# Making two decay tables on chip and reordering the first three blocks of a fused retention, mixture-of-experts and gated-MLP kernel

## Chip, cores and metric

One core of one Trainium2 chip. The metric is the device time of one launch in microseconds (us), the median of several runs. Three runs of the kernel before stand at the start of this case; the profile comes from one more execution.

## What is computed

Three stages, all float32, for 4 batches of 576 positions. Only the first matters here:

```python
scores = q @ k.T / sqrt(64)                       # 8 heads of 64
gamma  = 1 - 2.0 ** (-5 - arange(8))              # one decay per head
D      = where(t >= s, gamma ** (t - s), 0)       # causal decay mask
x      = (scores * D) @ v                         # then the heads side by side: 512 columns
# x -> top-1 mixture of experts (routing by x) -> gated MLP with a spatial product -> out
```

## The kernel before, in words

The first stage works on 16 blocks of 128 positions: block `j` is chunk `j // 4` of batch `j % 4`. (The last 64 positions of each batch come afterwards.) Each block is one tile of 128 x 2048 floats, loaded in two halves of 512 KB: first q and k (`blk[:, 0:1024]`), then k by rows and v. I call these halves a and b. Loads are issued on SP (SyncE's queue) by `load_blk`, and there are five block buffers (`bp`, tag "blk", line 271). The Tile framework puts the waits in.

For block `j` the steps are

- `scaled` (line 401, POOL): the keys times a table `ktab` (`kt`), and from chunk 1 on the queries times a table `q1`, `q2` or `q3` (`qh`);
- `scores` (line 370, PE): 16 small float32 products into the one PSUM tile `sc`. Every float32 product stands in the trace as two records, so these are 32;
- `masked` (line 391, DVE): two multiplications of `sc` by the mask table `dtab` (128 x 1024 floats, powers of gamma times 0.125 under the causal mask), giving `pm`;
- `state_products` and `score_products` (lines 466 and 476, PE): the running state times `qh`, and `pm` times v, into PSUM tile `oT`. For chunk 0 there is no state, and `state_products` issues nothing;
- `evict` (line 497, ACT): `oT` to `xT` in SBUF;
- `state_update` (line 412): PE products of `kt` and v into PSUM tile `st`, and DVE's addition to the state `Sbd`;
- `turn` (line 508, PE): `xT` times an identity beside the routing weights (`iw`) into PSUM tile `tx`; `logits` (DVE) and `keep` (ACT) read it.

The loop at line 777 sets the order. PE's order is exactly the order of the calls (`manual_schedule` for PE only); the orders on DVE, ACT, POOL and SP in this stretch are chosen by the framework's planner. In step `j` of the loop PE does `scores(j)`, `state_products(j-1)`, then `state_update(j-2)` and `turn(j-2)`, then `score_products(j-1)`. So the masked scores of a block have one step to be made before they are used. `routing` (line 604 and on) is fed in between by `advance`; after block 15 the routing of the last blocks ends the stage, and the expert products (lines 1179 to 1181) start at 114.37 us.

`small_constants` (line 329), called in step 1, loads a tile `CS` and copies ten small tables from it on DVE. `keep_warm` (line 252) issues bf16 products of a zero tile; seven of them stand ahead of the loop. The constant tables `dtab`, `q1` and the others are computed on the host into one array `cst`, and `load_c` loads a column range of it.

Of the kernel before, what the change touches and what calls it, by code (L numbers as in the profile page):

```python
# [8 lines left out]
F32 = mybir.dt.float32  # L9
# [5 lines left out]
ALU = mybir.AluOpType  # L15
# [4 lines left out]
B, H, S, DH = 4, 8, 576, 64  # L20
# [4 lines left out]
P = 128  # L25
NBLK = 18
TW = P + 9
# [4 lines left out]
EC = 256  # L32
HC = EC + CAPS[0]
GATE_TH = -1.788e-7
WARM = (4, 2, 3, 3)
FILL = (8, 3, 30, 48)
ET = mybir.EngineType
# [4 lines left out]
LPOOL = (1, 4, 6)  # L42

_CONST_LAYOUT = [
    ("dtab", H * P), ("q1", 4 * P), ("q2", 4 * P), ("q3", 4 * P), ("q4", 4 * P),
    ("late", H * 64),
    ("ktab", 4 * H), ("ident", P), ("jmat", 64), ("halfm", 2), ("first", 1), ("rest", 1), ("e8", 8),
    ("mless", 32), ("mmore", 32), ("rbase", 1), ("sel4", 4), ("i32", 32),
# [7 lines left out]
    _o += _w  # L56
CW = _o
SMALL0 = COFF["ident"][0]


def shape_constants(caps):
    c = np.zeros((P, CW), np.float64)

    def put(name, a, rows=P):
        o, w = COFF[name]
        c[:rows, o:o + w] = np.asarray(a, np.float64).reshape(rows, w)

    gam = 1.0 - 2.0 ** (-5.0 - np.arange(H))
    i = np.arange(P)
    rel = i[None, :] - i[:, None]  # L70
    dt = np.zeros((P, H, P))
    for h in range(H):
        g = np.where(rel >= 0, gam[h] ** np.maximum(rel, 0), 0.0) * 0.125
        dt[:, (h % 2) * 4 + h // 2] = np.roll(g, 64 * (h // 2 % 2), axis=0)
    put("dtab", dt)
    kt = np.zeros((P, 4, H))
    for cc in range(4):
        for h in range(H):
            kt[:, cc, h] = gam[h] ** (512.0 - cc * P - np.roll(i, 64 * (h // 2 % 2)))
    put("ktab", kt)  # L80
    qt = np.zeros((P, 3, 4, P))
    late = np.zeros((P, 2, 4, 64))
    q4 = np.zeros((P, 4, P))
    for pr in range(4):
        for hh in range(2):
            g = gam[2 * pr + hh]
            for cc in range(1, 4):
                qt[hh * 64:(hh + 1) * 64, cc - 1, pr, :] = 0.125 * g ** (cc * P + i - 512.0)
            late[:, hh, pr] = np.where(np.arange(64)[None, :] >= (i % 64)[:, None], g ** -(i % 64.0)[:, None], 0.0)
            q4[(hh ^ pr % 2) * 64:(hh ^ pr % 2) * 64 + 64, pr] = 0.125 * g ** (i % 64.0)  # L90
    for cc in range(3):
        put(f"q{cc + 1}", qt[:, cc])
    put("q4", q4)
    put("late", late)
    put("ident", np.eye(P))
    put("jmat", (i[:, None] % 64) == np.arange(64)[None, :])
    put("halfm", np.stack([i < 64, i >= 64], 1))
    put("first", (i == 0))
    put("rest", (i > 0))
    put("e8", np.tile(8.0 - np.arange(8), (P, 1)))  # L100
    rb, re = np.arange(32) // 8, np.arange(32) % 8
    same_e = re[:, None] == re[None, :]
    put("mless", same_e * (rb[:, None] < rb[None, :]), 32)
    put("mmore", same_e * (rb[:, None] > rb[None, :]), 32)
    put("rbase", RS * re - 1.0, 32)
    put("sel4", rb[:, None] == np.arange(4)[None, :], 32)
    put("i32", np.eye(32), 32)
    put("esum", re[:, None] == np.arange(8)[None, :], 32)
    put("row0", np.tile(RS * np.arange(8.0) - 1.0, (P, 1)))
    put("seq", np.tile(np.asarray(SEQ, np.float64), (P, 1)))  # L110
    put("iota_pb", np.arange(4)[None, :] * P + i[:, None] + 1.0)
    put("iota_bk", np.tile(np.arange(20.0) * P, (P, 1)))
    put("iota_p", i)
    put("caps", np.tile(np.asarray(caps, np.float64), (P, 1)))
    return c.astype(np.float32)


def lay_out(q, k, v, moe_w_gate, moe_w_local, moe_w1, moe_w2,
# [21 lines left out]
    for b in range(4):  # L140
# [14 lines left out]
    ws[64:, 4] = wt[512:]  # L155
    wo = moe2_w_out.reshape(4, P, 512).transpose(1, 0, 2).reshape(P, 2048)
    bs = np.tile(moe2_b_spatial[None, :], (P, 1))
    r = dict(blk=blk, lat=lat, wgl=wgl.reshape(P, 4 * TW), w1=w1, w2=w2, wv=wv, wu=wu,
             ws=ws.reshape(P, 5 * S), wo=wo, bs=bs, cst=shape_constants(caps))
    r = {n: np.ascontiguousarray(a) for n, a in r.items()}  # L160
    return {n: a.view(np.int64) if a.dtype == np.float64 else a for n, a in r.items()}


def fused(tc, blk, lat, wgl, w1, w2, wv, wu, ws, wo, bs, cst, out, dbg=None, stop=9, caps=CAPS):
    nc = tc.nc
    V, A, G, T, SP = nc.vector, nc.scalar, nc.gpsimd, nc.tensor, nc.sync
    top = ExitStack()
    with top:
# [100 lines left out]
        with ExitStack() as ph1:  # L269
# [22 lines left out]
                    SP.dma_start(out=ST[i][hf][oth].rearrange("p h c -> p (h c)"), in_=lat[i, oth, 1536:])  # L292

            CS = c1.tile([P, CW - SMALL0], F32, name="CS")
            CB = {n: c1.tile([P, COFF[n][1]], F32, name=f"c_{n}") for n in ("dtab", "q2", "late", "ktab")}
            iw = c1.tile([P, 4, TW], F32, name="iw")
            MV = [[c1.tile([P, H, DH], F32, name=f"mv{i}_{hf}") for hf in range(2)] for i in range(2)]
            LQ = [c1.tile([P, 1024], F32, name=f"lq{i}") for i in range(2)]
# [8 lines left out]
            def load_c(name):  # L307
# [2 lines left out]
                    CB[name] = c1.tile([P, w], F32, name="c_q")  # L310
                SP.dma_start(out=CB[name], in_=cst[:, o:o + w])

            load_blk(0, ((0, 1024),))
            load_c("dtab")
            load_blk(0, ((1024, BLKW),))
            load_c("ktab")
            load_blk(1, ((0, 1024),))
# [73 lines left out]
            def masked(j):  # L391
                d = blks[j]
                sc = d["sc"]
                tab = cs("dtab").rearrange("p (k a t) -> p k a t", k=2, a=4)
                d["pm"] = []
                for hh in range(2):
                    pm = wk.tile([P, 4, P], F32, name=f"pm{hh}")
                    V.tensor_tensor(pm, sc[:, hh], tab[:, hh], op=ALU.mult)  # L398
                    d["pm"].append(pm)

            def scaled(j):
                d = blks[j]
                if d["c"] > 0:
                    d["qh"] = wk.tile([P, 4, P], F32, name="qh", tag="qh")
                    tab = cs(f"q{d['c']}").rearrange("p (a t) -> p a t", a=4)
                    G.tensor_tensor(d["qh"], d["q"], tab, op=ALU.mult)
                kt = wk.tile([P, H, DH], F32, name="kt", bufs=3)
                ktb = cs("ktab").rearrange("p (c h) -> p c h", c=4)[:, d["c"]]
                G.tensor_tensor(kt, d["kk"], ktb[:, :, None].to_broadcast([P, H, DH]), op=ALU.mult)
                d["kt"] = kt  # L410
# [361 lines left out]
            order = tc.manual_schedule(engines={mybir.EngineType.PE})  # L772
            order.__enter__()
            V.memset(zb, 0.0)
            for n in range(7):
                keep_warm(sc_[:, n % 2], 1)
            for j in range(16):
                if j == 14:
                    order.__exit__(None, None, None)
# [5 lines left out]
                    load_late((j - 10) // 2)  # L785
                if j == 1:
                    small_constants()
                if j in (2, 5, 10, 11):
                    load_c({2: "q1", 5: "q2", 10: "q3", 11: "late"}[j])
                if j == 14:  # L790
                    for u in range(4):
                        load_w(u)
                views(j)
                scaled(j)
                scores(j)
                if j > 0:
                    state_products(j - 1)
                masked(j)
                advance()
                if j > 1:  # L800
                    state_update(j - 2)
                    turn(j - 2)
                    logits(j - 2)
                    keep(j - 2)
                    if j in (12, 13):
                        move_state(j - 10)
                    if j == 15:
                        round_w(0)
                        rest_w(0, G)
                if j > 1 and (j - 1) % 4 == 0:  # L810
                    steps.append(routing((j - 5) // 4))
                    advance()
                if j > 0:
                    score_products(j - 1)
                    evict(j - 1)
                advance()
# [739 lines left out]
        order.__exit__(None, None, None)  # L1556


_INS = ["blk", "lat", "wgl", "w1", "w2", "wv", "wu", "ws", "wo", "bs", "cst"]


# [16 lines left out]
```

## Time and profile before

| | |
|---|---|
| three runs, median (lowest to highest) | 562.27 us (560.90 to 562.31) |
| the profiled execution: its time, its span | 561.66 us, 559.9 us |
| instructions | 11740 |
| bytes read from and written to HBM | 77.34 MB, 18.91 MB |
| first stage, up to the first expert product | 114.37 us of the span |
| bytes moved in the first 110 us | 29.84 MB |

The span is what the profiler recorded from the first instruction to the last; the 1.8 us that the execution's time is longer lie around it. In timeline rows the columns are: start in us, duration in us, engine, line, operation, output and inputs with shapes, number of instructions merged into the row, and in brackets the idle time of the engine ahead of it and what ended it. "issue" there means that the profile shows nothing that the engine waited for. PE is the matmul side of TensorE, PEld its weight loads, SPq the loads issued by SP.

### The profile page before, as it was taken

The page shows a single profiled execution, that of the slowest core. Times are in us where ns is not written, and L with a number is a line of the kernel's source. Part 1 is how long each engine was busy: PE and PEld are TensorE (multiplying, and loading weights), DVE is VectorE, ACT ScalarE, POOL GpSimd, SP SyncE. Part 2 cuts the span into 40 slices and gives each one's busy share as a digit, 9 for nine tenths or more (in the row PEclk, how much of TensorE's full clock was granted, in tenths as well). Part 3 has the DMA queues.
Part 4 walks back from the last instruction along what each step waited for, and adds up shares of the span by engine and source line. Part 5 has one row for each costly group of instructions (what it writes and reads, how often), then busy time and mean ns, then how long its engine had stood idle before and what let it go on. Part 6 is the DMA issues. An engine that isn't in the chain of part 4 may idle for free.

```text
span 559.9 us, 11740 instructions
## 1 busy us (share of the span) xinstructions
PE 538.2 (96%) x4629; PEld 491.7 (88%) x4630; DVE 337.0 (60%) x713; ACT 223.4 (40%) x450; POOL 215.9 (39%) x176
## 2 busy tenths in 40 slices
PE   6898899899999999999999999999999899999997
PEld 4787777899999999999999998888888899889986
DVE  1566576533376778698875437996642846666510
ACT  1233243144455544555555542223333523662322
POOL 2566738445134636675635311322004244522000
PEclk9999999999999999999999999999999899999999
DMA  8989953537465474665565514353425553642022
GB/s 295 404 259 373 348 188 108 199 113 240 152 207 180 144 258 157 225 198 192 185 208 157 187 54 113 114 166 124 155 82 174 174 148 107 196 157 77 1 76 94
DMA packets 34059, 97.83 MB, mean 175 GB/s; under 512 B 5604, under 2 KB 5988, under 8 KB 34000
## 3 DMA queue, kind: packets, MB, share of 16 engines
q1 hardware_dynamic: 27696, 77.27, 41.2%
q0 software_dynamic: 5984, 19.24, 11.2%
q8 instruction: 37, 0.61, 0.5%
q10 hardware_dynamic: 320, 0.52, 0.3%
q14 instruction: 22, 0.18, 0.1%
HBM read 77.34 MB, written 18.91 MB: 172 GB/s over the span
## 4 chain that ended last, share of the span: by engine, by line
PE 69%; DVE 5%; ACT 2%; DMA 1%; issue 1%; POOL 0%; ACTq 0%; POOLq 0%; DVEq 0%; SPq 0%
PE acc L1179 12%; PE acc L1180 11%; PE acc L1181 11%; PE acc L1271 11%; PE acc L1273 11%; PE acc L1272 10%; PE tp L1157 1%; DVE wL L245 1%; PE tp L1439 1%; DMA vL<-z_v,yidx 1%; DVE ec L1009 1%; PE acc L1456 1%; PE acc L1455 1%; DVE hL L1198 1%; DVE bigL L1476 0%
## 5 line engine op out<-in xcount | busy, mean ns | idle before, releaser
L245 POOL TENSOR_TENSOR wL<-wst,wH 128x1024 fp32r<-128x1024 f32 x25 | 63.4, 2537 | 60.1 <-ACT wH L241 60.0
L1179 PE MATMUL acc<-hH,wH 128*128 128x416 f32 (+7 forms) x256 | 79.3, 310 | 0.1
L1180 PE MATMUL acc<-hL,wH 128*128 128x416 f32 (+7 forms) x256 | 78.0, 305 | 1.3 <-DVE hL L1198 1.3
L1181 PE MATMUL acc<-hH,wL 128*128 128x416 f32 (+7 forms) x256 | 77.9, 304 | 0.0
L245 DVE TENSOR_TENSOR wL<-wst,wH 128x1024 fp32r<-128x1024 f32 x39 | 52.3, 1342 | 39.3 <-ACT wH L241 38.3
L1180 PE MATMUL acc<-xL,wH 128*128 128x344 f32 (+6 forms) x224 | 66.7, 298 | 0.0
L1181 PE MATMUL acc<-xH,wL 128*128 128x344 f32 (+6 forms) x224 | 66.7, 298 | 0.0
L1179 PE MATMUL acc<-xH,wH 128*128 128x344 f32 (+6 forms) x224 | 66.5, 297 | 0.0
L241 ACT CAST wH<-wst 128x1024 fp32r<-128x1024 f32 x64 | 65.1, 1052 | 1.5 <-DMA wst<-in_w 1.5
L1180 PEld LDWEIGHTS acc<-hL,wH 128*128 128x128 f32 x256 | 48.2, 188 | 1.7 <-DVE hL L1198 1.7
L1179 PEld LDWEIGHTS acc<-hH,wH 128*128 128x128 f32 x256 | 48.2, 188 | 0.5 <-ACT hH L1197 0.3
L1181 PEld LDWEIGHTS acc<-hH,wL 128*128 128x128 f32 x256 | 48.1, 188 | 0.0
L1179 PEld LDWEIGHTS acc<-xH,wH 128*128 128x128 f32 x224 | 42.1, 188 | 0.0
L1181 PEld LDWEIGHTS acc<-xH,wL 128*128 128x128 f32 x224 | 42.1, 188 | 0.0
L1180 PEld LDWEIGHTS acc<-xL,wH 128*128 128x128 f32 x224 | 42.1, 188 | 0.0
L1271 PE MATMUL acc<-wsH,vH 128*128 128x288 f32 x128 | 39.0, 304 | 1.8 <-ACT ze L1383 1.7
L1273 PE MATMUL acc<-wsH,vL 128*128 128x288 f32 x128 | 38.4, 300 | 0.0
L1272 PE MATMUL acc<-wsL,vH 128*128 128x288 f32 x128 | 38.4, 300 | 0.0
L1197 ACT ACTIVATE hH<-acc 128x160 fp32r<-128x160 f32 (+7 forms) x64 | 24.8, 400 | 31.4 <-PE acc L1181 31.2
L1198 DVE SCALAR_TENSOR_TENSOR hL<-acc,hH 128x160 fp32r<-128x160 f32 (+7 forms) x64 | 27.5, 440 | 14.1 <-ACT hH L1197 13.6
L1276 POOL DMA_INDIRECT vL<-z_v,yidx x18 | 17.6, 980 | 44.8 <-DMA z_v<-ze 40.4
L398 DVE TENSOR_TENSOR pm<-sc,c_dtab 128x512 f32<-128x512 f32 x32 | 20.6, 685 | 22.7 <-PE sc L376 22.7
(286 smaller groups left out, 1314.9 us busy)
## 6 DMA issues: line engine op xcount, KB each, us to landing
wst<-in_w SPq DMA_DIRECT2D x64, 512.0 KB, 3.6
blk<-in_blk SPq DMA_DIRECT2D x32, 512.0 KB, 8.5
z_v<-ze SPq DMA_DIRECT2D x18, 257.0 KB, 2.8
z_u<-ze SPq DMA_DIRECT2D x18, 256.0 KB, 2.4
out<-ob SPq DMA_DIRECT2D x15, 256.0 KB, 2.0
raw<-in_wv SPq DMA_DIRECT2D x4, 512.0 KB, 5.0
raw<-in_wu SPq DMA_DIRECT2D x4, 512.0 KB, 5.1
raw<-in_wo SPq DMA_DIRECT2D x4, 512.0 KB, 5.2
```

What stands on the lines that cost most here:

```text
L241: A.copy(wts[u][0], stages[u])
L245: eng.tensor_tensor(wL, stages.pop(u), wH.bitcast(F32), op=ALU.subtract)
L398: V.tensor_tensor(pm, sc[:, hh], tab[:, hh], op=ALU.mult)
L1179: T.matmul(acc, lhsT=wH, rhs=xH, start=first, stop=False)
L1180: T.matmul(acc, lhsT=wH, rhs=xL, start=False, stop=False)
L1181: T.matmul(acc, lhsT=wL, rhs=xH, start=False, stop=last)
L1197: A.activation(hH[:, cols], acc[:, :C], AF.Relu)
L1198: V.scalar_tensor_tensor(hL[:, cols], acc[:, :C], 0.0, hH[:, cols].bitcast(F32), op0=ALU.max, op1=ALU.subtract)
L1271: T.matmul(acc, lhsT=lH, rhs=rH, start=first, stop=False)
L1272: T.matmul(acc, lhsT=lH, rhs=rL, start=False, stop=False)
L1273: T.matmul(acc, lhsT=lL, rhs=rH, start=False, stop=last)
L1276: G.indirect_dma_start(out=t.bitcast(F32), out_offset=None, in_=src[:], in_offset=bass.IndirectOffsetOnAxis(ap=yidx[:, j:j + 1], axis=0))
```

## The change

On chip: the mask table `dtab` and the query table `q1` are no longer loaded. A tile of 8 rows (one per head) and 1792 columns, `rt8`, holds powers of gamma and 0/1 selectors; it is loaded first, into one of the five block buffers, and a 128 x 64 tile of zeros and ones (`mask`) is loaded after the first half of block 0. Eight float32 products of 8 rows make gamma^(t-s) in PSUM; four DVE multiplications by `mask` and two ACT copies carry it into a `dtab` tile that POOL has set to zero. In step 1 four products make `q1`, which ACT copies out.

Order: four instead of seven `keep_warm` ahead of the loop; then block 0 is carried up to `evict` in step 0 (with seven and one `keep_warm` around its products), and its state update, `turn`, `logits` and `keep` move from step 2 to step 1. From block 1 on, the products stay where they were.

```diff
-    ("dtab", H * P), ("q1", 4 * P), ("q2", 4 * P), ("q3", 4 * P), ("q4", 4 * P),
+    ("mask", 64), ("q2", 4 * P), ("q3", 4 * P), ("q4", 4 * P),
...
+TROW = H * P + 512 + 256
...
+def row_tables():
+    gam = 1.0 - 2.0 ** (-5.0 - np.arange(H))
+    i = np.arange(P)
+    t = np.zeros((H, TROW), np.float64)
+    keys, sel = t[:, :H * P].reshape(H, H, P), t[:, H * P:H * P + 512].reshape(H, 4, 2, 64)
+    for h in range(H):
+        keys[h, h] = gam[h] ** -np.roll(i, 64 * (h // 2 % 2)).astype(np.float64)
+        sel[h, h // 2, h % 2] = 1
+    t[:, -256:-128] = 0.125 * gam[:, None] ** i[None, :]
+    t[:, -128:] = 0.125 * gam[:, None] ** (P + i[None, :] - 512.0)
+    return t.astype(np.float32)
...
+            rt8 = bp.tile([P, BLKW], F32, name="rt8", tag="blk")[:H, :TROW]
+            SP.dma_start(out=rt8, in_=rowt)
             load_blk(0, ((0, 1024),))
-            load_c("dtab")
+            load_c("mask")
             load_blk(0, ((1024, BLKW),))
...
             V.memset(zb, 0.0)
-            for n in range(7):
+            dtab = c1.tile([P, H * P], F32, name="dtab")
+            q1 = c1.tile([P, 4 * P], F32, name="c_q")
+            G.memset(dtab, 0.0)
+            for n in range(START[0]):
                 keep_warm(sc_[:, n % 2], 1)
+            dt = psc.tile([P, 2, 512], F32, name="oT")
+            for h in range(H):
+                T.matmul(dt[:, h % 2, h // 2 * P:(h // 2 + 1) * P], lhsT=rt8[:, h * P:(h + 1) * P],
+                         rhs=rt8[:, TROW - 256:TROW - 128], start=True, stop=True)
+            dt, tab = (t_.rearrange("p k (a o s t) -> p k a o s t", a=2, o=2, s=2)
+                       for t_ in (dt, dtab.rearrange("p (k x) -> p k x", k=2)))
+            mask = cs("mask")[:, None, None, :].to_broadcast([P, 2, 2, 64])
+            for o in range(2):
+                for kh, sl in enumerate(both[::1 - 2 * o]):
+                    V.tensor_tensor(tab[sl, :, :, o, kh], dt[sl, :, :, o, kh], mask[sl], op=ALU.mult)
+                A.copy(tab[both[o], :, :, o, 1], dt[both[o], :, :, o, 1])
             for j in range(16):
...
-                if j in (2, 5, 10, 11):
-                    load_c({2: "q1", 5: "q2", 10: "q3", 11: "late"}[j])
+                if j in (5, 10, 11):
+                    load_c({5: "q2", 10: "q3", 11: "late"}[j])
...
+                if j == 1:
+                    qp = pso.tile([P, 2, 512], F32, name="tx")[:, 0]
+                    for pr in range(4):
+                        at = H * P + pr * P
+                        T.matmul(qp[:, pr * P:(pr + 1) * P], lhsT=rt8[:, at:at + P], rhs=rt8[:, TROW - 128:],
+                                 start=True, stop=True)
+                    A.copy(q1, qp)
                 views(j)
                 scaled(j)
                 scores(j)
-                if j > 0:
+                if j > 1:
                     state_products(j - 1)
                 masked(j)
                 advance()
-                if j > 1:
+                if j == 0:
+                    keep_warm(psc.tile([P, 512], F32, name="warm", tag="st"), START[1])
+                    state_products(0)
+                    score_products(0)
+                    evict(0)
+                    keep_warm(psc.tile([P, 512], F32, name="warm", tag="st"), START[2])
+                if j == 1:
+                    state_update(0)
+                    turn(0)
+                    logits(0)
+                    keep(0)
+                if j > 2:
                     state_update(j - 2)
                     turn(j - 2)
...
-                if j > 0:
+                if j > 1:
                     score_products(j - 1)
                     evict(j - 1)
```

`START` is `(4, 7, 1)`. `masked` and `scaled` read the tiles `dtab` and `q1`; the new input `rowt` holds `row_tables()`.

## Rows read from the trace of the kernel before

**Rows 1.** The page, part 1: busy us of each engine, share, instructions

```profile
PE 538.2 (96%) x4629; PEld 491.7 (88%) x4630; DVE 337.0 (60%) x713; ACT 223.4 (40%) x450; POOL 215.9 (39%) x176
```

**Rows 2.** Timeline of PE, 0 to 22 us

```profile
1.04 3.17 PE L254 MATMUL sc<-zb 128*128 128x512 bf16 x7 [1.04 <-DVE one L930]
5.13 1.56 PE L376 MATMUL sc<-blk 64*64 64x128 f32 x32 [0.92 <-DMA blk<-in_blk]
10.22 1.56 PE L376 MATMUL sc<-blk 64*64 64x128 f32 x32 [3.53 <-DMA blk<-in_blk]
11.71 1.82 PE L481 MATMUL oT<-pm,blk 128*64 128x128 f32 x16
13.48 0.90 PE L376 MATMUL sc<-blk 64*64 64x128 f32 x32
14.31 0.69 PE L423 MATMUL st<-blk,kt 128*64 128x64 f32 x16
...
15.77 1.04 PE L481 MATMUL oT<-pm,blk 128*64 128x128 f32 x16
16.74 0.90 PE L376 MATMUL sc<-blk 64*64 64x128 f32 x32
...
19.38 0.92 PE L519 MATMUL tx<-iw,xT 128*64 128x137 f32 x12 [0.88 <-issue]
```

**Rows 3.** Windows of 5 us: busy by engine, granted clock, DMA share, GB/s

```profile
5.00:10.00 5.00, 1.56 (x32) 1.36 (x32) 1.29 (x2) 0.00 (x0) 1.04 (x1) 1.00 1.01 366
```

**Rows 4.** Windows between PE's unexplained stops, same columns

```profile
0.00:18.50 18.50, 13.00 (x219) 9.77 (x221) 5.26 (x15) 3.12 (x6) 5.64 (x15) 1.00 0.90 323
18.50:25.10 6.60, 5.65 (x125) 5.08 (x125) 3.92 (x16) 2.34 (x6) 4.43 (x4) 1.00 1.03 405
```

**Rows 5.** DMA queues, 16 to 17 us: packets, MB, share

```profile
q8 instruction: 1, 0.02, 6.3%
```

**Rows 6.** Timeline of PE at the end of the first stage

```profile
111.75 0.48 PE L712 MATMUL sc<-identR,xg 32*128 32x32 f32 x4 [1.01 <-DMA xg<-x_sorted,gidx]
```

**Rows 7.** Timeline of SP's loads, 0 to 12 us

```profile
0.78 0.39 SPq L285 DMA_DIRECT2D blk<-in_blk  x1
1.22 0.42 SPq L311 DMA_DIRECT2D c_dtab<-in_cst  x1
...
10.97 1.43 SPq L285 DMA_DIRECT2D blk<-in_blk  x2
```

**Rows 8.** DMA issues at 0.78, 1.22, 2.16, 3.36: KB, us to landing

```profile
blk<-in_blk SPq DMA_DIRECT2D x1, 512.0 KB, 4.3
c_dtab<-in_cst SPq DMA_DIRECT2D x1, 512.0 KB, 5.4
c_ktab<-in_cst SPq DMA_DIRECT2D x1, 16.0 KB, 6.0
iw<-in_wgl SPq DMA_DIRECT2D x1, 274.0 KB, 7.4
```

**Rows 9.** The page, part 6: issues, KB each, us to landing

```profile
z_u<-ze SPq DMA_DIRECT2D x18, 256.0 KB, 2.4
```

**Rows 10.** Timeline: one full-array float32 product, one ACT copy, POOL's memsets

```profile
94.76 0.99 PE L725 MATMUL tx<-identR,xge 128*128 128x128 f32 x8
...
16.87 0.59 ACT L503 COPY xT<-oT 128x512 f32<-128x512 f32 x1
...
0.78 1.06 POOL L346 MEMSET Sbd<- 128x256 f32 x4 [0.29 <-POOLq L1567]
```

**Rows 11.** Timeline of DVE, 0 to 22 us

```profile
6.77 1.29 DVE L398 TENSOR_TENSOR pm<-sc,c_dtab 128x512 f32<-128x512 f32 x2 [5.77 <-PE sc L376]
...
15.67 0.41 DVE L431 TENSOR_TENSOR Sbd<-Sbd,st 128x256 f32<-128x256 f32 x1
...
17.69 0.17 DVE L332 COPY rt<-CS 128x8 f32<-128x8 f32 x1 [1.50 <-DMA CS<-in_cst]
...
18.99 1.27 DVE L398 TENSOR_TENSOR pm<-sc,c_dtab 128x512 f32<-128x512 f32 x2
```

More of the change, by code (lines that the diff above doesn't have):

```diff
@@ L34 @@
 GATE_TH = -1.788e-7
+START = (4, 7, 1)
 WARM = (4, 2, 3, 3)
@@ L69, in shape_constants @@
     i = np.arange(P)
[L70 to L75, printed above, removed]
+    put("mask", np.arange(64)[None, :] >= (i % 64)[:, None])
     kt = np.zeros((P, 4, H))
@@ L86, in shape_constants @@
             g = gam[2 * pr + hh]
-            for cc in range(1, 4):
+            for cc in range(2, 4):
                 qt[hh * 64:(hh + 1) * 64, cc - 1, pr, :] = 0.125 * g ** (cc * P + i - 512.0)
@@ L90, in shape_constants @@
             q4[(hh ^ pr % 2) * 64:(hh ^ pr % 2) * 64 + 64, pr] = 0.125 * g ** (i % 64.0)
-    for cc in range(3):
+    for cc in range(1, 3):
         put(f"q{cc + 1}", qt[:, cc])
@@ L157, in lay_out @@
     bs = np.tile(moe2_b_spatial[None, :], (P, 1))
-    r = dict(blk=blk, lat=lat, wgl=wgl.reshape(P, 4 * TW), w1=w1, w2=w2, wv=wv, wu=wu,
+    r = dict(blk=blk, lat=lat, rowt=row_tables(), wgl=wgl.reshape(P, 4 * TW), w1=w1, w2=w2, wv=wv, wu=wu,
              ws=ws.reshape(P, 5 * S), wo=wo, bs=bs, cst=shape_constants(caps))
@@ L161, in lay_out, with fused @@
     return {n: a.view(np.int64) if a.dtype == np.float64 else a for n, a in r.items()}
-def fused(tc, blk, lat, wgl, w1, w2, wv, wu, ws, wo, bs, cst, out, dbg=None, stop=9, caps=CAPS):
+def fused(tc, blk, lat, rowt, wgl, w1, w2, wv, wu, ws, wo, bs, cst, out, dbg=None, stop=9, caps=CAPS):
     nc = tc.nc
@@ L294, in fused @@
             CS = c1.tile([P, CW - SMALL0], F32, name="CS")
-            CB = {n: c1.tile([P, COFF[n][1]], F32, name=f"c_{n}") for n in ("dtab", "q2", "late", "ktab")}
+            CB = {n: c1.tile([P, COFF[n][1]], F32, name=f"c_{n}") for n in ("mask", "q2", "late", "ktab")}
             iw = c1.tile([P, 4, TW], F32, name="iw")
@@ L393, in masked @@
                 sc = d["sc"]
-                tab = cs("dtab").rearrange("p (k a t) -> p k a t", k=2, a=4)
+                tab = dtab.rearrange("p (k a t) -> p k a t", k=2, a=4)
                 d["pm"] = []
@@ L404, in scaled @@
                     d["qh"] = wk.tile([P, 4, P], F32, name="qh", tag="qh")
-                    tab = cs(f"q{d['c']}").rearrange("p (a t) -> p a t", a=4)
+                    tab = (q1 if d["c"] == 1 else cs(f"q{d['c']}")).rearrange("p (a t) -> p a t", a=4)
                     G.tensor_tensor(d["qh"], d["q"], tab, op=ALU.mult)
@@ L1556, in fused @@
         order.__exit__(None, None, None)
-_INS = ["blk", "lat", "wgl", "w1", "w2", "wv", "wu", "ws", "wo", "bs", "cst"]
+_INS = ["blk", "lat", "rowt", "wgl", "w1", "w2", "wv", "wu", "ws", "wo", "bs", "cst"]
 def kernel(**inputs):
```

## Prediction

> **What bounds the kernel now.** I read the page's busy shares first: PE is at work for 96% of the span [rows 1], so time is won where PE stands still, or where it does something that need not be done. Then the timeline of PE over the first 22 us, the stretch that the change touches. There PE stands still twice for data: 0.92 us ahead of block 0's scores and 3.53 us ahead of block 1's [rows 2]. In those first microseconds the loads set the pace: between 5 and 10 us the DMA engines are busy all the time, at 366 GB/s [rows 3]. The second thing to see is PE's speed. The products of one block (L481, 16 records) take 1.82 us at 11.71 and 1.04 us at 15.77 [rows 2]: until about 13.4 us PE works at the lower of its two levels (1.2 GHz), then at 2.4 GHz, although the granted-clock column reads 1.00 all the way [rows 3, 4]. It rose after some 3.2 us without a pause, from 10.22 on.
>
> From 13.48 us PE waits for no data of a block any more. What is left are stops that the profile calls "issue", 0.88 us at the first of them [rows 2]. Up to that stop there are 219 PE records and 221 weight loads, and from it to the next 125 and 125 [rows 4], 250 instructions; two microseconds ahead of the stop one packet of 0.02 MB comes over the instruction queue [rows 5]. I read these stops as PE running out of instructions while the next packet stands behind the data. The stage ends with the routing of the last tokens; PE's last wait there is for rows gathered from memory [rows 6], at the end of a chain that starts from block 15's logits. That chain hangs on PE's position and not on a load of the start, so a lead that PE has at 20 us should be kept to the end of the span.
>
> **Loads.** Gone: `dtab`, 524,288 bytes, ahead of block 0's second half, and `q1`, 262,144 bytes, behind block 4. New: `rt8`, 8 x 1792 x 4 = 57,344 bytes, and `mask`, 32,768 bytes. Ahead of block 1 that is 434,176 bytes less; at 366 GB/s [rows 3] 1.2 us. SP issues one load per 0.44 us [rows 7]; `rt8` goes first, so block 0's first half, landing at 0.78 + 4.3 = 5.1 [rows 8], comes 0.4 later, at 5.5. Block 1's first half comes between 9.0 and 9.5 in place of 10.2. `mask` lands behind block 0's half as `ktab` does behind its predecessor (1.70 + 6.2 = 7.9 for that one, 2.16 + 6.0 = 8.2 for `ktab` [rows 8]): 0.3 us behind, 5.9. `rt8` itself finds an empty queue; the nearest row is 2.4 us for 256 KB [rows 9], so it lands at 3.2, or 2.8 if its few bytes help. Its buffer is block 4's: that load is issued at 10.97 now [rows 7], and cannot be before the `q1` products are done, near 11.1 by the sum below. What stands behind it on SP (block 4's halves, then block 5) is not needed before about 19 us, so I cost that at nothing; if the `q1` products came 2 us later, it would begin to show.
>
> **The table, built.** Eight products are 16 records. No row shows one of 8 rows; bounds: 0.065 us a record, as for the half-width product (1.04 / 16 [rows 2]), 1.0 in all, and 0.124 (0.99 / 8, full width [rows 10]) times 1.75 for the lower clock (1.82 / 1.04), 3.5 in all. The weights are full width, so I go by that row and take the lower clock for the first half: 2.6 us, from 3.2 to 5.8. Then DVE: four multiplications of 256 columns out of PSUM, 0.41 each as the nearest such row [rows 11]: 1.6 us from 5.9 (mask and table both there) to 7.5. ACT's two copies (under 0.59 each [rows 10]) lie beside these, and POOL's memset of 1024 columns is the 1.06 us that four of 256 take [rows 10], done by 3.1 behind those. `masked(0)` takes 1.29 [rows 11]: it starts at 7.5, now at 6.77, and ends at 8.85.
>
> **PE, step 0.** Four warming products (3.17 / 7 = 0.45 each [rows 2]) end at 2.85; the table 3.2 to 5.8; scores(0), 0.90 to 1.56 [rows 2], at the higher clock, since PE has hardly paused since 1.04: 6.7. Seven warming products at half of 0.45 each: 8.3. They are filler in a wait for DVE, so they cost nothing as long as the clock is up; at the lower clock they and scores(0) end at 10.5, and products(0) is 1.6 us later. That is one end of my range. products(0) wait for `masked(0)`: 8.9 to 9.9, and one more warming product to 10.1.
>
> **PE, step 1.** The `q1` products, 8 records, 1.0 us by the same row [rows 10] (0.5 to 1.7): 11.1. scores(1), their data there since 9.5, 0.90: 12.0. State update and turn of block 0 as now from 14.31 to 15.77 [rows 2], 1.46: 13.5. `iw` has landed (3.36 + 7.4 = 10.8 before [rows 8], earlier now), `evict(0)` and the copy of `q1`, 0.59 each [rows 10], are done by 11.7.
>
> **PE, steps 2 and 3.** scores(2) 13.5 to 14.4. Here the change adds a wait: `sc` is one tile, `masked(2)` takes until 15.75, and only products(1), 1.0 us, now lie between scores(2) and scores(3). So scores(3) start at 15.75 rather than 15.4, and end at 16.65. Before they end at 16.74 + 0.90 = 17.64 [rows 2], with the same work done. Gain so far: **1.0 us**.
>
> **The stop.** Ahead of the first stop there are now 4 + 16 + 7 + 1 + 8 = 36 fillers and table records in place of 7: 29 more. It falls inside scores(3), and its packet, asked for earlier by about the 2.5 us that PE is ahead in record count, should come no later against PE than now. I give it 0 to 0.5 us in favour, 0.2. Sum: 1.2 us.
>
> The Trainium skill, "Runtime: NRT & Kernel Launch", section "Instruction fetch mechanics", says that instructions come in blocks of 16 KiB, 256 of them, and that crossing into the next is mostly hidden. The block agrees with the rows (250 instructions, 0.02 MB [rows 4, 5]); "hidden" does not: 0.88 us [rows 2]. By the page the sum would be 1.0, by the rows 1.2.
>
> **Sum.** The profiled execution took 561.66 us; 561.66 - 1.2 = 560.5. It lies 0.6 below the median of the runs shown, so against that it is 561.1; I give **560.7**. About 0.3%, 1.7 us, can be told from no change here.
>
> **Rivals.**
> - *More than that.* The table's products cost 0.065 a record: the table is done at 4.2, but `mask` still gates DVE at 5.9; the `q1` products are 0.5 shorter, the lead is 1.5, and a stop that vanishes adds 0.7: 2.2 us, 559.5. For it: only 8 of 128 rows are loaded. Against: the weights are as wide as in the row of 0.124.
> - *Given back to the instruction packets.* While the DMA engines are full, PE gets 250 instructions per 6.6 us [rows 4] whatever it does, and 29 records more have to pass. 29 of 125 is 0.23 of 6.6, 1.5 us against the lead of 2.5 in record count, minus what the stop already costs: gain 0 to 0.6, 561.4.
> - *Slower: DVE behind the constants.* The planner, not the kernel, places the ten copies out of `CS` on DVE. Today they stand between block 0's logits and `masked(3)`, and wait 1.50 us for the load, to 17.69; then `masked(3)` begins at 18.99 [rows 11]. If they now stand ahead of `masked(2)`, that one waits until about 16.5 (17.6 less 1.1) + 1.3 = 17.8, scores(3) until 19.1, ending at 20.0 in place of 17.64: 2.4 us late, of which up to 1.0 comes back because the stop lies in that wait. 1.4 to 2.4 us slower, 563.5. It decides if `CS` lands later than scores(2) end (14.4) and the copies go first.
> - *The change does nothing.* If the lower clock holds through step 0, products(0) end at 12.3 at 1.82 us, the `q1` products run slow too (1.7), and scores(1) end at 14.9: the lead is gone, 562.
>
> **How the numbers follow.** The sum as worked, 0.4 to 2.2 us gained: 0.54 (0.16 of it past 1.7). More: 0.20. Packets: 0.10. No lead from the clock: 0.05. DVE behind the constants and its like: 0.11. Faster by over 0.3%: 0.16 + 0.20 + a little, 0.37; slower by over 0.3%: 0.11 and half of the clock case's tail, 0.13; the rest, 0.50, within. Range: 558.9 (a gain of 2.8) to 563.2 (the cheap end of the slower case).
>
> **What would show it.** Right: on PE's timeline scores(1) at 10.5 to 11.5 taking 0.90 us; products(0) ahead of them at 1.04; scores(3) ending 0.6 to 1.6 us earlier than 17.64; the first expert product at about 113.2. The table: 16 records from about 3.2, four DVE rows of 0.41 ending near 7.5. Wrong: L481 still at 1.82; scores(3) waiting for DVE with a row "CS" ahead; stops of more than 0.9 us; or a lead at 20 us that is gone at 114.

## The result, and the profile after

Slower. The kernel after takes 564.06 us (median of 15 runs) against 561.63 us for the kernel before beside it: ratio **1.0053**, 95% interval 1.0036 to 1.0070, or 3.0 us more (2.0 to 3.9). The prediction was 560.7 us, a gain. The profiled execution after took 564.38 us, its span 562.6; before it was 561.66 and 559.9. One run before and two after, 12 us longer than the others, are left out of the ratio, and the profiled execution of r13_zeros below was such a long one too.

PE's timeline of the kernel after, 0 to 24 us (columns as in [rows 2]):

```profile
1.04 1.89 PE L264 MATMUL sc<-zb 128*128 128x512 bf16 x4 [1.04 <-DVE zb L786]
3.26 3.78 PE L794 MATMUL oT<-rt 8*128 8x128 f32 x16 [0.34 <-DMA rt<-in_rowt]
6.97 1.56 PE L388 MATMUL sc<-blk 64*64 64x128 f32 x32
8.46 3.17 PE L264 MATMUL warm<-zb 128*128 128x512 bf16 x7
11.83 1.68 PE L493 MATMUL oT<-pm,blk 128*64 128x128 f32 x16 [0.20 <-DVE pm L410]
13.45 0.39 PE L264 MATMUL warm<-zb 128*128 128x512 bf16 x1
13.77 1.15 PE L823 MATMUL tx<-rt 8*128 8x128 f32 x8
14.85 0.90 PE L388 MATMUL sc<-blk 64*64 64x128 f32 x32
...
17.24 0.90 PE L388 MATMUL sc<-blk 64*64 64x128 f32 x32
18.07 1.09 PE L493 MATMUL oT<-pm,blk 128*64 128x128 f32 x16
19.57 0.90 PE L388 MATMUL sc<-blk 64*64 64x128 f32 x32 [0.40 <-DVE pm L410]
...
22.83 0.90 PE L388 MATMUL sc<-blk 64*64 64x128 f32 x32
```

What PE's timeline loses, it loses in the first 15 us. The eight table products (L794) take 3.78 us, scores(0) 1.56, the seven zeros 3.17: every row up to 11.63 has the duration of the lower clock, although PE hardly pauses. Products(0) begin at 11.83, and scores(1) at 14.85 against 10.22 [rows 2]. From there to scores(3) the distances are those that the prediction worked out (4.72 us here, 4.65 there). Scores(4) start 1.7 us later than before (22.83; before 21.10, of which 0.88 us is the stop at 19.38 [rows 2]). Scores(3), ahead of that stop, start 2.8 us later (19.57; before 16.74).

DVE and ACT in the same kernel, DVE first, 7 to 13 us:

```profile
7.14 0.86 DVE L801 TENSOR_TENSOR dtab<-oT,c_mask 64x256 f32<-64x256 f32 x2 [6.15 <-PE oT L794]
9.80 0.86 DVE L801 TENSOR_TENSOR dtab<-oT,c_mask 64x256 f32<-64x256 f32 x2 [1.80 <-ACT dtab L802]
11.09 1.29 DVE L410 TENSOR_TENSOR pm<-sc,dtab 128x512 f32<-128x512 f32 x2 [0.43 <-ACT dtab L802]
```

```profile
8.11 1.28 ACT L802 ACT_TABLE_LOAD   x1 [7.97 <-DVE dtab L801]
9.40 0.37 ACT L802 COPY dtab<-oT 64x256 f32<-64x256 f32 x1
10.69 0.37 ACT L802 COPY dtab<-oT 64x256 f32<-64x256 f32 x1 [0.92 <-DVE dtab L801]
```

The two engines take turns: two multiplications, a copy, two multiplications, a copy, then `masked(0)`. They write different parts of one tile, `dtab`, and each waits for the other. The first turn also holds ACT's table load of 1.28 us, the first instruction of ACT's work, which now waits for DVE (7.97 us of idle time; in the kernel before it ran at 0.78). From the first multiplication to `masked(0)` it is 3.95 us.

The loads. The windows of 4 to 8 us, 15 to 25 and 105 to 110 of the kernel after, then the first two of the kernel before (columns as in [rows 3]); last, SP's wait at the `q1` products and its load rows:

```profile
4.00:8.00 4.00, 4.00 (x41) 3.77 (x43) 0.84 (x2) 0.00 (x0) 0.00 (x0) 1.00 0.95 259
...
15.00:25.00 10.00, 9.60 (x254) 8.67 (x252) 7.66 (x22) 2.92 (x7) 5.09 (x5) 1.00 0.94 298
105.00:110.00 5.00, 5.00 (x34) 4.80 (x33) 3.92 (x25) 0.00 (x0) 2.00 (x3) 0.73 0.41 157
```

```profile
4.00:8.00 4.00, 1.77 (x33) 1.36 (x32) 1.23 (x2) 0.00 (x0) 0.00 (x0) 1.00 1.01 358
15.00:25.00 10.00, 9.12 (x209) 8.18 (x206) 5.92 (x22) 3.47 (x9) 6.11 (x6) 1.00 1.03 405
```

```profile
SPq L295 <- PE tx L823: 4.2, 1, 4.2
```

```profile
1.25 0.37 SPq L295 DMA_DIRECT2D blk<-in_blk  x1
...
9.88 0.78 SPq L343 DMA_DIRECT2D x_sorted<-in_wgl  x1
14.95 2.44 SPq L295 DMA_DIRECT2D blk<-in_blk  x4
```

Block 0's half is issued at 1.25 and lands 5.2 us later (the view of issues), at 6.45; it was 5.1 before [rows 8]. SP stands from 10.66 to 14.95 for the buffer that `rt8` holds, and the transfer rate from 15 to 25 us is 298 GB/s instead of 405.

At the end of the stage the first expert product starts at 118.79 us, 4.4 later than before. Part of that is not the change's: from 105 to 110 us the granted clock was 0.73, and the records of L758 stand 0.21 us apart from 104.1 to 107.6 instead of 0.12, some 1.5 us. Such dips, to between 0.5 and 0.9 over 5 us, came at various places in every profile below, none of them before 30 us, so the start of scores(4), ahead of all of them, is the landmark that I compare.

### The profile page after: what moved, and what is told of

Read it like the earlier page. It is cut to its first block, busy times and chain, and to the rows that moved or that the text cites. A ratio compares the mean times of both kernels' runs of the same rounds, so it can differ in the third digit from the quotient of the medians.

```text
span 562.6 us, 11805 instructions
## 1 busy us (share of the span) xinstructions
PE 544.4 (97%) x4658; PEld 495.6 (88%) x4659; DVE 339.3 (60%) x717; ACT 224.8 (40%) x453; POOL 216.9 (39%) x177
## 4 chain that ended last, share of the span: by engine, by line
PE 71%; DVE 4%; ACT 2%; issue 1%; ACTq 0%; DVEq 0%
PE acc L1315 11%; PE acc L1223 11%; PE acc L1316 11%; PE acc L1317 11%; PE acc L1224 11%; PE acc L1225 11%; PE tp L1201 1%; DVE wL L255 1%; PE tp L1483 1%; DVE ec L1053 1%; PE acc L1499 1%; PE acc L1500 1%; DVE hL L1242 1%; DVE bigL L1520 0%; DVE sb L1516 0%
## 5 line engine op out<-in xcount | busy, mean ns | idle before, releaser
L1263 ACT COPY yT<-acc 128x160 f32 (+7 forms) x32 | 12.5, 392 | 53.5 <-PE acc L1225 53.4
```

Of the source, the lines that this page charges most:

```text
L1263: A.copy(yT[d // 3][:, d % 3, bass.ds(at, caps[r])], acc[:, C - caps[r]:C])
```

## The experiments

Twelve kernels were run. "Start of scores(4)" is from each one's profile (before 21.10, after 22.83); ratios are to the kernel before, with 95% intervals.

| kernel | ratio | scores(1) start | scores(4) start |
|---|---|---|---|
| after | 1.0053 (1.0036 to 1.0070) | 14.85 | 22.83 |
| r1_order | 0.9970 (0.9941 to 0.9998) | 10.07 | 19.79 |
| r9_order0 | 0.9970 (0.9956 to 0.9985) | 10.38 | 20.00 |
| r13_zeros | 0.9987 (0.9966 to 1.0008) | 10.51 | 20.09 |
| r10_delay | 0.9996 (0.9982 to 1.0010) | 10.52 | 20.70 |
| r12_products | 1.0017 (0.9997 to 1.0038) | 12.41 | 20.83 |
| r5_hand | 1.0010 (0.9984 to 1.0037) | 14.07 | 22.05 |
| r4_own | 1.0017 (0.9991 to 1.0044) | 14.97 | 22.95 |
| r8_best | 1.0022 (0.9995 to 1.0049) | 13.85 | 22.71 |
| r11_table_hand | 1.0024 (1.0005 to 1.0044) | 11.07 | 21.59 |
| r2_table | 1.0031 (0.9999 to 1.0063) | 12.99 | 23.16 |
| r6_hand_fill | 1.0040 (1.0009 to 1.0072) | 13.46 | 21.43 |
| r7_wide | 1.0049 (1.0025 to 1.0074) | 14.83 | 23.38 |

### The two halves of the change, each alone

r1_order is the kernel before with the new order of block 0 and three zeros in place of seven in step 0; both tables are loaded as before. r2_table is the kernel after with the old order.

```diff
 # r1_order, in the loop of the kernel before; START is (7, 3, 1)
...
+                if j == 0:
+                    keep_warm(psc.tile([P, 512], F32, name="warm", tag="st"), START[1])
+                    state_products(0)
+                    score_products(0)
+                    evict(0)
+                    keep_warm(psc.tile([P, 512], F32, name="warm", tag="st"), START[2])
+                if j == 1:
+                    state_update(0)
+                    turn(0)
+                    logits(0)
+                    keep(0)
...
```

> The kernel before, its two tables loaded as ever, with the new order of blocks 0 to 2 alone (seven products of zeros ahead of the loop, three and one around block 0's products). Theory (the making of the tables at the start costs the time, the order by itself is good): the products of block 0 run from about 8.1 to 9.9 us, block 1's scores start at 10.2 as before, block 3's scores end near 16.8 in place of 17.64, and the kernel is 0.5 to 1.5 us faster than before. Rival (the order costs it, by the short step between block 2's and block 3's scores and by other instruction stops): block 3's scores end at 19 or later and the kernel is 1.5 to 3 us slower than before.

> The changed kernel with the order of before: the two tables made on chip, four products of zeros ahead, nothing else moved. Theory: the mask table is not ready before 11 us, so block 0's masked scores end at 12.4 and block 1's scores start there or later, not at 10.2; block 3's scores end at 19.5 to 20.5 and the kernel is 2 to 3.5 us slower than before. Rival (the order costs the time): block 3's scores end at about 17.6 and the kernel is within 1 us of before.

PE of r1_order, then of r2_table:

```profile
8.17 1.09 PE L482 MATMUL oT<-pm,blk 128*64 128x128 f32 x16 [1.36 <-DVE pm L399]
9.20 0.39 PE L255 MATMUL warm<-zb 128*128 128x512 bf16 x1
10.07 0.90 PE L377 MATMUL sc<-blk 64*64 64x128 f32 x32 [0.48 <-DMA blk<-in_blk]
```

```profile
12.99 1.56 PE L388 MATMUL sc<-blk 64*64 64x128 f32 x32 [2.39 <-DVE pm L410]
```

The order alone is a gain, 0.9970: products(0) go into the wait for block 1. The table alone is a loss by the middle of its interval, 1.0031 (0.9999 to 1.0063): scores(1) wait for the masked scores of block 0. So the change is a good half and a bad half. In r1_order scores(3) end at 17.13 (16.8 expected, 17.64 before), in r2_table at 20.79, a little past the 19.5 to 20.5 expected. Both together (1.0053) are worse than the sum of both alone (1.0001, give or take 0.0043), just beyond the noise; why is not shown, for scores(4) start 0.3 us earlier in the kernel after than in r2_table.

### The hand-offs between DVE and ACT

r5_hand changes two things in the kernel after: ACT copies one small number at the start, so that its table load comes there, and all four multiplications go ahead of both copies.

```diff
+            early_ = c1.tile([32, 1], F32, name="early")
             G.memset(dtab, 0.0)
+            A.copy(early_, carF)
...
             for o in range(2):
                 for kh, sl in enumerate(both[::1 - 2 * o]):
                     V.tensor_tensor(tab[sl, :, :, o, kh], dt[sl, :, :, o, kh], mask[sl], op=ALU.mult)
+            for o in range(2):
                 A.copy(tab[both[o], :, :, o, 1], dt[both[o], :, :, o, 1])
```

> The changed kernel with ACT's function table loaded at the start (a copy of 32 values that waits only for POOL) and the four DVE multiplications of the table ahead of both ACT copies, so that the work changes hands once instead of three times. Theory (the hands and the table load are on the path, but the seven products of zeros at the lower clock are just as long): the mask table is ready at 9.7 in place of 11.06 and block 0's masked scores at 11.0 in place of 12.38, but PE is at its zeros until 11.6, so block 0's products start only 0.2 us earlier and the time is within 0.6 us of the changed kernel. Rival (the hands alone cost the time): block 1's scores start 1.3 us or more earlier than 14.85 and the kernel is at least 1 us faster than the changed one.

DVE, then ACT, of r5_hand:

```profile
7.22 1.63 DVE L803 TENSOR_TENSOR dtab<-oT,c_mask 64x256 f32<-64x256 f32 x4 [6.23 <-PE oT L796]
9.74 1.29 DVE L410 TENSOR_TENSOR pm<-sc,dtab 128x512 f32<-128x512 f32 x2 [0.89 <-ACT dtab L805]
```

```profile
0.78 1.28 ACT L791 ACT_TABLE_LOAD   x1 [0.65 <-PEq L1614]
...
8.96 0.74 ACT L805 COPY dtab<-oT 64x256 f32<-64x256 f32 x2 [6.70 <-DVE dtab L803]
```

`masked(0)` starts at 9.74 instead of 11.09, and the ratio falls from 1.0053 to 1.0010 (the intervals all but part). But products(0) now start at 11.64, with no wait for DVE: only 0.2 earlier, since the seven zeros at the lower clock end just then. Scores(4) come 0.8 earlier; the other 0.6 of it is that products(0) took 1.09 us here and 1.68 in the kernel after, the clock having risen by then. The place came as the theory had it (0.2 us at products(0)), the time did not: by the ratios it is 2.4 us under the kernel after, give or take 1.8, where at most 0.6 was expected and the timeline shows 0.8 at scores(4). What the rest is, no run says. r6_hand_fill takes that second chain away as well, with three zeros in place of seven.

> The run with ACT's table load at the start and one change of hands, now with three products of zeros between block 0's scores and its products instead of seven. In the run with seven, the masked scores were ready at 11.03 us and PE was at the zeros until 11.63. Theory (zeros and table are two chains side by side, and both must be shortened): block 0's products start at 11.1 and, since the clock is still at its lower level or only just up, end between 12.1 and 12.9; block 1's scores start at 13.5 or a little later in place of 14.07, block 3's scores end at 18.5 to 19.7, time within 1 us of that run. Rival (the zeros are what holds the clock up and fewer of them cost more than they save): block 0's products take 1.6 us or more and block 1's scores start at 14.0 or later.

PE of r6_hand_fill:

```profile
10.44 0.43 PE L493 MATMUL oT<-pm,blk 128*64 128x128 f32 x2 [0.48 <-DVE pm L410]
11.03 1.09 PE L493 MATMUL oT<-pm,blk 128*64 128x128 f32 x14 [0.17 <-DVE pm L410]
```

Scores(1) come 0.6 earlier than in r5_hand, scores(4) 0.6. In the time it does not show: 1.0040, 1.7 us above r5_hand where the two were expected within 1 us, with an interval that holds r5_hand's ratio. The same mend in the old order, r11_table_hand, is r2_table with the edit of r5_hand.

> The table kernel in the old order (1.0031) with ACT's table load early and the four multiplications ahead of ACT's two copies. If the hand-offs between DVE and ACT are what holds scores(1) there (pm(0) not done before 12.4, scores(1) start 12.99), pm(0) is done near 11, scores(1) start 11.2 to 11.8 and scores(3) end 19.0 to 19.6 (20.79 without the mend); ratio 1.000 to 1.002. If PE itself holds it (products at the lower clock), scores(3) end moves by less than 0.4 and the ratio stays at 1.003.

Scores(1) start at 11.07 instead of 12.99, scores(4) 1.6 earlier: by place the hand-offs held scores(1) there too. The ratio went from 1.0031 only to 1.0024, and the intervals overlap; the runs do not show this gain in the time (1.000 to 1.002 was expected).

### PE's work on the table, without the hand-offs

r12_products is r1_order (both tables loaded) with the rows loaded as well and the eight products in place of three of the seven zeros. Nothing reads the products.

```diff
-            for n in range(7):
+            for n in range(4):
                 keep_warm(sc_[:, n % 2], 1)
+            dt = psc.tile([P, 2, 512], F32, name="oT")
+            for h in range(H):
+                T.matmul(dt[:, h % 2, h // 2 * P:(h // 2 + 1) * P], lhsT=rk8[:, h * P:(h + 1) * P],
+                         rhs=rs8[:, 512:640], start=True, stop=True)
...
```

> The new order with the tables loaded as before (0.997 so far), but four zeros and the eight 8-row products ahead of scores(0) in place of seven zeros; nothing reads the products, so no hand-off between DVE and ACT is left, only PE's work on the table and the loads of the rows. Theory A (the table costs by PE's work at the lower clock): products 3.3 to 7.1, scores(0) 1.56 to 8.6, products(0) at the lower clock or the zeros in front of them ending near 11, scores(1) 12.5 to 13.5, ratio 1.000 to 1.002. Theory B (it costs by the hand-offs): scores(1) before 12, scores(3) end under 18, ratio 0.996 to 0.999.

PE of r12_products:

```profile
3.31 3.75 PE L797 MATMUL oT<-rs,rk 8*128 8x128 f32 x16 [0.38 <-DMA rs<-in_rowt]
6.99 1.56 PE L394 MATMUL sc<-blk 64*64 64x128 f32 x32
8.48 1.46 PE L269 MATMUL warm<-zb 128*128 128x512 bf16 x3
9.88 2.06 PE L499 MATMUL oT<-pm,blk 128*64 128x128 f32 x16
11.87 0.61 PE L269 MATMUL warm<-zb 128*128 128x512 bf16 x1
12.41 1.10 PE L394 MATMUL sc<-blk 64*64 64x128 f32 x32
```

DVE's `masked(0)` starts at 8.63 here, the table being loaded, and still scores(1) start at 12.41: PE has no idle time from 3.31 on and works at the lower clock until then. The ratio, 1.0017, is 0.0047 above both order kernels: 2.6 us, give or take 1.4 (against r9_order0, from the two intervals). Theory A's numbers hold, scores(1) coming 0.1 us ahead of its range; PE's work on the products, with the load of their rows, turns the gain of the order into none.

r7_wide lays the same products out as two of 512 columns instead of eight of 128 (and `q1` as one of 512 instead of four), to see whether it is the number of instructions and weight loads that costs.

> The changed kernel with its small products laid out wide: one set of 8 x 128 weights against 8 x 1024 columns (two products of 512 columns in place of eight of 128), and one product in place of four for q1; all else as in the changed kernel. Theory: a weight load per 128 columns is what makes them slow at the lower clock, so the mask products take about 1.8 us instead of 3.78 and end near 5.2, q1's take 0.5 to 0.9 instead of 1.15; but the 0/1 tile lands only at 6.67, so the DVE steps start there, 0.5 us earlier than 7.14, and block 3's scores end at 19.3 to 20.1 in place of 20.47; time 0 to 1.5 us below the changed kernel. Rival (the length of the mask products was the main cost): block 3's scores end before 18.8 and the kernel is as fast as before or faster.

PE of r7_wide:

```profile
3.28 3.78 PE L795 MATMUL oT<-rt 8*128 8x512 f32 x4 [0.36 <-DMA rt<-in_rowt]
```

3.78 us, as with sixteen records: the price is that of 2048 columns of float32 records, 0.236 us per 128. My expectation of 1.8 us fell, and the ratio, 1.0049, is that of the kernel after.

r13_zeros is r1_order with twelve zeros ahead of scores(0) in place of seven.

> The same, with twelve zero products instead of seven ahead of scores(0) and no 8-row products: they end at 6.5 if the clock stays low, at 5.5 if it rises after the first seven. If PE's clock rises on zeros as it does not on the 8-row products, scores(0) takes 0.90 and scores(1) starts at 10.0 to 10.5, held by the load, ratio 0.996 to 0.999, though scores(0) is late by up to 1 us. If the clock stays low in step 0 whatever stands there, scores(0) takes 1.56 and scores(1) starts after 11.5.

PE of r13_zeros (the granted clock of its first 25 us, the part read here, is 1.00):

```profile
1.04 4.53 PE L255 MATMUL sc<-zb 128*128 128x512 bf16 x12 [1.04 <-DVE one L942]
5.51 0.90 PE L377 MATMUL sc<-blk 64*64 64x128 f32 x32
...
10.51 0.90 PE L377 MATMUL sc<-blk 64*64 64x128 f32 x32 [0.88 <-DMA blk<-in_blk]
```

After twelve zeros scores(0) run at 2.4 GHz (0.90), and a scores(0) that is 0.3 us later costs nothing, since the load of block 1 sets scores(1).

### What the clock of step 0 is worth, and what a delay does

r9_order0 is r1_order without any zeros in step 0; r10_delay is the kernel before with twenty more zeros behind scores(0), meant to make PE late by 2 to 4 us and nothing else.

> The order alone, the tables loaded, with no products of zeros inside the first step (seven ahead of the loop as before). Theory (the zeros there only fill a wait and keep the clock up): block 0's products run at the higher clock all the same or at most 0.8 us longer, block 1's scores start at 10.1 as with them, for they wait for their data; block 3's scores end at 16.9 to 17.8; time within 1 us of the order alone with three and one. Rival (the zeros are what makes the order good): the clock is at its lower level again from block 0's products to block 2's scores, block 3's scores end after 18, and the gain is gone.

> The kernel before with twenty more zero products behind scores(0): nothing else is changed, no table is made, no load moves; PE is only late by some 2 to 4 us at scores(1) (start near 13, before 10.22; scores(3) end 19.5 to 21, before 17.64). Theory A (a lag of PE at 20 us is kept to the end): first expert product late by the same amount, ratio 1.004 to 1.006. Theory B (the stops for instructions behind it give part of a lag back): the stops up to 91 us sum to less than the 5.0 of before, and the ratio is 1.001 to 1.003, under half of the lag at 20 us.

PE of r9_order0, then of r10_delay:

```profile
5.18 1.56 PE L377 MATMUL sc<-blk 64*64 64x128 f32 x32 [0.97 <-DMA blk<-in_blk]
8.24 1.97 PE L482 MATMUL oT<-pm,blk 128*64 128x128 f32 x16 [1.50 <-DVE pm L399]
10.38 1.56 PE L377 MATMUL sc<-blk 64*64 64x128 f32 x32 [0.16 <-DMA blk<-in_blk]
```

```profile
5.27 0.90 PE L376 MATMUL sc<-blk 64*64 64x128 f32 x32 [1.06 <-DMA blk<-in_blk]
6.10 4.49 PE L254 MATMUL warm<-zb 128*128 128x512 bf16 x20
10.52 0.90 PE L376 MATMUL sc<-blk 64*64 64x128 f32 x32
...
13.56 0.90 PE L376 MATMUL sc<-blk 64*64 64x128 f32 x32 [1.11 <-DMA blk<-in_blk]
```

r10_delay did not make the delay: in the profiled execution PE was at 2.4 GHz, the twenty zeros took 0.22 us each instead of 0.45 and ended at 10.5, when the data of block 1 was there. So it does not tell its two theories apart. It shows another thing. PE was at the upper level from 5.27 on, and won nothing (0.9996), as scores(2) then waited 1.11 us for their load. And r9_order0 worked at the lower level until past 13 us and is no slower than r1_order. So with the tables loaded PE's clock in step 0 is worth little: scores(4) start at 19.79 in r1_order and at 20.00 in r9_order0, as the loads set the pace there. With the tables made on chip PE has no idle time left, and the clock moves what follows: the 0.6 us that products(0) were shorter in r5_hand came back in full at scores(4).

### The buffer, and the best repair

r4_own keeps the rows in two weight buffers instead of block 4's, so that SP is not held. r8_best puts the mends together: the wide rows, ACT's table load early, copies ahead of multiplications, the `q1` product in step 0, and two zeros.

> The changed kernel with the 8-row tile in two buffers of its own (weight buffers that are free until 59 us) instead of a block buffer, so that block 4's load does not wait for the q1 products. Theory: SP's wait of 4.2 us at 10.7 goes and block 4 lands about 4 us earlier, but nobody waited for block 4, so block 3's scores end within 0.6 us of the changed kernel's 20.47 and the time is within 0.8 us of the changed kernel. Rival (the held buffer is a main cost): the first expert product comes 1.5 to 3 us earlier than the changed kernel's 118.79 and the kernel is about as fast as before.

> All mends together: wide products, ACT's table load at the start, ACT's two copies ahead of the four DVE multiplications (they need no 0/1 tile), q1's product ahead of block 0's products so that SP is not held, and two products of zeros in place of seven. Theory: the mask table is ready near 8.4 us, block 0's masked scores at 9.7, its products end near 10.9, block 1's scores start near 11.2, block 3's scores end at 16.3 to 17.3, about where the order alone has them (17.13); the kernel is 0.5 to 2 us faster than before. Rival (the tables on chip lose whatever is done, by the blocks' later landing): block 3's scores end after 18 and the kernel is slower than before.

In r4_own SP's wait of 4.2 us at the `q1` products is gone, but SP waits longer for the older block buffers, 22.8 us in ten waits for `st` against 17.8 in seven; scores(4) start at 22.95, no earlier, and scores(3) end at 20.59, as the theory had it. But the first expert product starts at 116.32, 2.5 us earlier than in the kernel after, as the rival had it, with dips of the clock ahead of it in both profiles. The ratio, 1.0017 against 1.0053, has intervals that overlap. What the held buffer costs stays open. r8_best has its table ready for `masked(0)` at 9.68, and then products(0) start at 11.40, behind the `q1` product (2.07 us from 8.44) and two zeros, all at 1.2 GHz: 1.0022. Scores(1), expected near 11.2, start at 13.85, and the gain of 0.5 to 2 us that was expected did not come. No version with the table on chip came out faster than the kernel before. r9_order0 beats both kernels: 559.96 us against 561.53 before, with an interval that lies wholly under 1 and under that of the kernel after.

## Why the prediction was wrong

**The sum failed in step 0 alone, by 3.75 us.** Scores(1) were put at 11.1 us and came at 14.85; from there on the sum holds.

- *The clock* (scores(0) "at the higher clock, since PE has hardly paused since 1.04"). This step failed. PE did not pause from 3.26 to 11.63 and stayed at the lower level. I had taken from [rows 2] that 3.2 us without a pause had raised it in the kernel before, and made a rule of one rise. The Trainium skill, "TensorE: Matmul & The Clock Gate", section "What's actually happening", has the clock go by how busy PE has been. PE's busy column is full, 4.00 of 4.00 us from 4 to 8, and the rows stay at the lower level up to 11.63: by that column this trace disagrees. Why the clock stayed low is open. The price is on the rows: the products 3.78 us against the 2.6 taken (2.7 by the row I used; the end of my bounds with the lower clock all through was 3.5), scores(0) 1.56 against 0.90, the zeros 3.17 against 1.6. So the zeros ended at 11.63 and not at 8.3. Of "They are filler in a wait for DVE, so they cost nothing as long as the clock is up" the condition was false. I gave this case a chance of 0.05 and 562 us; its landmarks were products(0) ending at 12.3 and scores(1) ending at 14.9 (here 13.51 and 15.75). The 562 was too low by these landmarks themselves: scores(1) ending 2.9 us behind the 12.0 of the sum turn its gain of 1.0 us at scores(3) into a loss of 1.9.
- *The table behind the products* ("ACT's two copies ... lie beside these"). This failed too, on its own: 7.14 to 11.06 instead of 5.9 to 7.5. I counted the instructions and not the order that one shared tile puts on two engines, and did not ask what stood ahead of ACT's first copy. By the table's two chains, mending this alone could move products(0) by 0.2 us only (next point).
- *The two together.* The zeros end at 11.63 and the first half of `pm` comes 0.20 later: either alone would have held products(0) to within 0.2 us of where they were. r5_hand shows it for the zeros (fewer zeros with the hand-offs as they were was not run), and r6_hand_fill for both, where both are shortened and scores(1) come 1.4 us earlier than after (14.85 to 13.46; 0.6 of it the clock, as in r5_hand).
- *Loads.* The rows came as taken (products at 3.26). Block 0's half was put at 5.5 and landed at 6.45, at 259 GB/s instead of 358 from 4 to 8 us. It hid behind the table products, which ended at 7.04. That the 0.43 MB less ahead of block 1 would let it come earlier was of no use, as nothing waited for it.
- *Block 4's buffer* ("if the `q1` products came 2 us later, it would begin to show"). They came 3.7 us later, SP stood for 4.2 us, and the transfers fell behind; only a part of that can be the buffer's, as r4_own, without that wait, moves 341 GB/s from 15 to 25 us. PE's places in r4_own up to scores(4) do not show it.
- *Steps 1 to 3*: right. `q1` products 1.15 (1.0 taken), scores(3) wait 0.40 us for `masked(2)` as worked out, and the ten copies out of `CS` did not go ahead of it: the slower rival that I priced at 563.5, DVE behind the constants, did not happen, though its time is near the one measured.
- *The order*: right in its direction. With the table its gain was taken as 1.0 us plus 0.2; alone it gave 1.7 us (0.8 to 2.5, by r9_order0). At scores(3), where the 1.0 was worked out, it is only 0.5 us in r1_order and 0.2 in r9_order0; what the rest of the 1.7 is, the places do not say.
- *A lead at 20 us is kept to the end*: borne out on the average only. Over the thirteen kernels of the table and the one before, a straight line of ratio x 561.6 us against the start of scores(4) has a slope of 0.99 us per us, with a correlation of 0.83. Single kernels lie up to 1.7 us off it. The kernel after is 1.0 us above: late by 1.7 us there, by 3.0 (2.0 to 3.9) in the end. The stop of 0.88 us in the 21.10 of the kernel before can be a part of that: at scores(3), ahead of it, the kernel after is late by 2.8. A single profile need not keep a lag: in r2_table scores(4) start 2.1 us late but the first expert product only 0.2 (114.53 against 114.37), with no dip of the clock up to there in either profile, and stops of 2.3 us up to 91 us against 5.0. r10_delay was meant to test this and did not.
- *The stops for instructions* ("It falls inside scores(3)", 0.2 us in favour). Not so: the stop at 19.38 is gone in the kernel after, where the first one comes at 26.79; in the twelve others the first comes anywhere from 20.5 to 61.5 us. After, the stops up to 91 us sum to 6.0 us, against 5.0 before and 2.3 to 4.4 in the twelve others; they differ from one execution to the next, so I put no price on this.

In the ratios the account is: order -1.7 us, PE's eight products +2.6, the rest of the table (hand-offs, more zeros, `q1`, the buffer) +2.0, which is 0.0036 between r12_products and the kernel after; each with 0.8 to 1.5 us either way. By the start of scores(4) the same three are -1.1 (0.88 of it is the stop of the kernel before), +0.8 and +2.0 us. In r2_table, with the table alone, it is a loss as well, if hardly clear of noise. What moved the end is shown, then, as the table on chip (0.9970 without it, 1.0053 with it); how much of it falls to each part is known to 0.8 to 1.5 us, and within the rest the hand-offs and the buffer are not told apart (1.0010 in r5_hand, 1.0017 in r4_own).

## What to carry to other kernels

Replacing a load by work on chip pays only if the engine that does the work stands idle there for as long; here PE had 3.5 us of waits to fill, and the new order and the new table were both meant to live on them. Price early TensorE work at the clock that the rows next to it show, and ask what the sum becomes if it does not rise. When two engines fill one tile in turns, cost the turns one after the other, and look at what the first instruction of each drags behind its wait.

## What the runs showed of the hardware that was not expected

- Float32 products with 8 rows cost 0.236 us per 128 columns and record at the lower level, in sixteen records or in four, and 0.14 at the upper one (1.15 / 8), no less than the 0.124 of a product with all 128 rows [rows 10].
- The upper level came at different times in like streams. With zeros alone ahead of scores(0), it was there by 5.5 us in r1_order, r10_delay and r13_zeros, and not before 13 us in the kernel before and r9_order0. With the 8-row products it was absent at scores(0) in nine profiles of nine. One profile each; whether these products keep the clock down is not settled.
- ACT's table load of 1.28 us can land behind a wait. In the kernel before it ran at 0.78, although the copy that it goes with (L503) waited until 13.58; in the kernel after it ran at 8.11, behind a wait for DVE that is an instruction of its own (8.0). One early copy brought it back to 0.78 (r5_hand).
